# Filters laid out by a copy in DRAM, and an inverse row product summed on VectorE between two exchanges of partitions

## The chip, the core and the metric

One core of one Trainium2 chip. The metric is the device time of one execution in microseconds (us); the median of three runs of the kernel before is 204.33 us (204.27 to 204.45).

## What is computed

The input x has 2048 rows of 640 numbers in bf16. It is normalised row by row; two branches take the normalised rows, and their results are added to x. Branch A is a filter in the frequency domain: a real two-dimensional Fourier transform (2048 x 321 complex values), a product with complex weights w_r + i w_i of that size, and the inverse transform. Branch B is a gated layer with 1536 hidden units.

```python
def _A_ref(x, w_r, w_i):
    X = rfft2(x.astype(float32), axes=(-2, -1))
    X = X * (w_r + 1j * w_i)
    return irfft2(X, s=(S, D), axes=(-2, -1)).astype(bfloat16)

def _B_ref(x, w_gate, w_up, w_down):
    h = einsum("bsd,df->bsf", x, w_gate) * einsum("bsd,df->bsf", x, w_up)
    return einsum("bsf,fd->bsd", h, w_down)

xn = _layernorm(x)
return x + _A_ref(xn, A_w_r, A_w_i) + _B_ref(xn, B_w_gate, B_w_up, B_w_down)
```

## The kernel before

The kernel is a list of tasks, and a planner written in Python orders them before the program is built. Each task has an engine (or a choice of engines), a planned duration, buffers that it reads and writes, and a priority; a lower number is more urgent. The planner (`_Sched.plan`) runs through a model of the five engines, picks the next task by start time and priority, and fixes for every engine the order in which it issues. The chip keeps that order: an instruction that waits on a semaphore holds everything behind it on its engine. All ordinary DMAs are issued from SyncE (SP) by the helper `dma` at L712; evictions of PSUM by ACT or DVE are all recorded at L718 and L719, the two branches of `copy_on`.

Rows are split over partitions as 128 x 16 row blocks b. The work runs in these stages, which overlap:

- *Normalisation.* Statistics of each block, then a subtraction (L824) and a product (L831, task `mul`), in place. From block 4 on, the normalised block is transposed by a DMA within SBUF (L837, issued from SP); the first four blocks are transposed on PE.
- *Branch B, first half.* L978 and L998 multiply the transposed blocks by gate and up weights (five matmuls of 512 columns at L978 for one hidden tile and one of the two weights), ACT or DVE evict, and DVE multiplies the two (L1014). It works on blocks 0 to 3, then 4 to 7, 8 to 11 and 12 to 15. Its priority is 40, so that PE does it whenever nothing more urgent is ready.
- *Branch A, forward.* DVE does a part of the transform along the columns (L891 to L925), PE the next (L938). When all blocks are there, the row stage begins: for t = 0 to 15, two matrices of matmuls (task D, L1056), evictions of 64 partitions, then task C (L1079) with two groups g = 0, 1 of 321 columns each.
- *Filter product, inverse rows.* DVE multiplies C's PSUM output by the filter's real and imaginary part (task WM: two instructions at L1094 and one at L1097 per group) into the buffer Y. The negated parts are made by NG (L1107, on POOL, ACT or DVE) and NS (L1114 to L1116, on POOL). Task IA (L1130, L1131) then needs two accumulating matmuls for each of five parts of each group: one with the product, one with the negated and exchanged product. Its result is evicted into Z2. Y has three buffers.
- *Filters.* For every second t, three or four DMAs for each of w_r and w_i load four frequency rows straight from the weight in DRAM into one of three SBUF slots, repeated and reversed as the 128 partitions need them. They wait for the last block's `mul`.
- *Inverse columns and output.* I (L1159) needs all of Z2; DVE combines (L1183 to L1216). For each block a and half, ACC (L1237) sums branch B's second product over twelve hidden tiles into a PSUM bank, IV (L1249) adds branch A into that bank, FIN (L1257, DVE) adds x, and a DMA stores the half.

Of the kernel before, what the change touches and what calls it, by code (L numbers as in the profile page):

```python
# [398 lines left out]
def _build_tables():  # L399
# [27 lines left out]
    fd = np.zeros((128, 4 * 128 + 130), np.float64)  # L427
# [25 lines left out]
    t["fd"] = _bf16_bits(fd)  # L453
    t["g"] = _bf16_bits(gd)
# [5 lines left out]
    npm = np.repeat(np.arange(2), _S1)  # L460
    nk1 = np.tile(np.arange(_S1), 2)
    n_re = 64 * npm + 2 * nk1
    n_im = n_re + 1
    tf = np.zeros((128, _NQ, 128), np.float64)
    ti = np.zeros((128, _NQ, 2, 64), np.float64)
    for q in range(_NQ):
        k = _rows(q, npm, nk1)
        ph = two_pi * ((s1[:, None] * k[None, :]) % _S) / _S
        c = np.exp(-1j * ph)
        pm = np.broadcast_to(npm[None, :], (64, 64))  # L470
# [9 lines left out]
        ti[n_re, q, 0] = im.real  # L480
        ti[n_im, q, 0] = -im.imag
        ti[n_re, q, 1] = im.imag
        ti[n_im, q, 1] = im.real
# [3 lines left out]


def _rows(q, pm, k1):
    lo = np.where(pm == 0, q, np.where(q == 0, _R // 2, _R - q))  # L490
    return lo + _R * k1
# [11 lines left out]
_WD_LOADS = ((7, 12), (0, 2), (2, 4), (4, 6), (6, 7))  # L503
_FT_ORDER = (7, 8, 9, 10, 11, 0, 1, 2, 3, 4, 5, 6)
# [5 lines left out]
_YS = 1090  # L510
_NY = 3
# [39 lines left out]
def _build(nc, A_x, A_w_r, A_w_i, B_w_gate, B_w_up, B_w_down, out, opts=None):  # L551
# [3 lines left out]
    with es:  # L555
# [6 lines left out]

        sch = _Sched()
# [27 lines left out]
        lay["TI"] = (lay["WD"][0], 16 * 256)  # L591
# [20 lines left out]
        b_y = alloc("Y", _NY * 2 * _YS)  # L612
# [29 lines left out]
        v_w = V("W").rearrange("p (r w n) -> p r w n", r=2, w=2)  # L642
        v_wr = [v_w[:, 0], v_w[:, 1], V("W3").rearrange("p (w n) -> p w n", w=2)]
        b_wr = [(b_w, 0), (b_w, 16), (b_w3, 0)]
# [5 lines left out]
        v_ti = V("TI").rearrange("p (q c n) -> p q c n", q=_NQ, c=2)  # L650
        v_wd = V("WD").rearrange("p (f d) -> p f d", f=12)
        v_fd = V("FD")
        v_g = V("G")
# [11 lines left out]
        v_y = V("Y").rearrange("p (r g n) -> p r g n", r=_NY, g=2)  # L665
        v_tc2 = V("TC").bitcast(_F32).rearrange("p (r s u n) -> p r s u n", r=2, s=5, u=2)
# [19 lines left out]
        v_sd = arena[:, o_stat + 432: o_stat + 448]  # L686
        b_st = sch.buf("st", 10 ** 9, 1)
# [35 lines left out]
        dma("ld_fd", v_fd[:, 0:642], d_fd, 128 * 1284, [(b_fd, None)], prio=0.3)  # L723
# [240 lines left out]
        for ui, (at_, ci, ft0) in enumerate(units):  # L964
# [7 lines left out]
            for u in range(2):  # L972
                ft = ft0 + u
                if nb == 4:
# [10 lines left out]

                    def em_eg4(c, gu=gu, rr=rr, u=u):
                        return copy_on(c, v_gbf[:, rr, u, :], ps[:, bank_of(gu), :])
# [24 lines left out]
            def em_h(c, ft0=ft0, rr=rr, n=n, rows=rows, nb=nb):  # L1012
                if nb == 4:
                    return c.e.tensor_tensor(v_ht[:, ft0, rows], v_gbf[:, rr, 0, :], v_gbf[:, rr, 1, :], _OP.mult)  # L1014
                return c.e.tensor_tensor(v_ht[:, ft0:ft0 + 2, rows], v_gbf[:, rr, :, 0:n], v_gbf[:, rr, :, n:2 * n],
                                         _OP.mult)
            T("H_%d" % ui, "dve", _d_dve_tt16(min(2 * n, 512)), em_h,
# [4 lines left out]
        for q in range(2):  # L1022
            dma("ld_ti%d" % q, v_ti[:, 16 * q:16 * q + 16], d_ti[:, 16 * q:16 * q + 16], 128 * 8 * 512,
                [(b_wd, ("e", 2048 * q, 2048 * q + 2048))], prio=9.0 + 0.3 * q, after=[muls[opts.get("w_after", 15)]])

        for t in range(16):
# [4 lines left out]
            if t % (_WQ // 2) == 0:  # L1031
                q0 = 2 * t
                for w_ in range(2):
                    wv, dw = wvs[w_], v_wr[wr][:, w_]
                    parts = [(dw[0:64], wv[:, q0:q0 + _WQ, :].rearrange("k1 q l -> k1 (q l)").unsqueeze(1).to_broadcast(
                        [_S1, 2, _WQ * 321]), 64 * _WQ * 642)]
                    o_ = 0
                    if q0 == 0:
                        o_ = 1
                        parts.append((dw[64:128, 0:321], wv[:, _R // 2, :].unsqueeze(1).to_broadcast([_S1, 2, 321]), 64 * 642))  # L1040
                    for d_ in range(2):
                        parts.append((dw[64 + d_:128:2, 321 * o_:321 * _WQ].rearrange("p (q l) -> p q l", l=321),
                                      wv[:, _R - q0 - o_:_R - q0 - _WQ:-1, :], 32 * (_WQ - o_) * 642))
                    for i_, (dst, src_, nb_) in enumerate(parts):
                        dma("ld_w%d_%d_%d" % (t, w_, i_), dst, src_, nb_,
                            [(b_wr[wr][0], ("r", b_wr[wr][1] + 8 * w_ + 2 * i_, b_wr[wr][1] + 8 * w_ + 2 * i_ + 2))],
                            prio=9.5 + 0.05 * t, semkey=("w", wr), after=[muls[opts.get("w_after", 15)]])

            eds = []
# [23 lines left out]
            for g in range(2):  # L1073
                q = 2 * t + g
                pg = pq + 0.0005 * g
                ys = 2 * yr + g

                def em_c(c, q=q, g=g, ar=ar):
                    return c.e.matmul(ps[:, bank_of(c.t), 0:_LP], v_tf[:, q, :], v_a[:, ar, 324 * g:324 * g + _LP],  # L1079
                                      start=True, stop=True)  # L1080
                tc = T("C_%d" % q, "pe", _d_mm(_LP), em_c, reads=[(b_a, ("r", 2 * ar, 2 * ar + 2)), (b_tf, ("t", t, t + 1))],
                       prio=pg, bank="single", cls="b")

# [266 lines left out]
```

## Time and profile before

| what | value |
|---|---|
| median of three runs | 204.33 us |
| span of the profiled execution (its own time in the profile) | 202.8 us |
| what the median holds beyond that span | 1.5 us |
| PE, DVE, ACT, POOL busy | 198.0, 179.5, 127.5, 32.0 us |
| bytes moved by DMA | 23.82 MB |
| row stage, from D's first matmul to I's first | 82.6 to 140.1 us |
| first product with a filter (L1094) | 86.5 us |
| first inverse matmul (L1130) | 90.3 us |

The span runs from the first to the last instruction. A busy time is the union of an engine's records; records of PE matmuls overlap, so that the mean of a record (196 ns for 64 columns) is longer than the distance between two. A DMA's time to landing runs from its issue until its data are there. The DMA share is the mean busy share of the core's 16 DMA engines.

### The profile page before, as it was taken

Reading aid. Unit: us, or ns where it says so; the run is one execution under the profiler, and the core shown is the slowest. Engines: PE = TensorE matmul, PEld = TensorE weight load, DVE = VectorE, ACT = ScalarE, POOL = GpSimd, SP = SyncE. Lnnn points to the kernel's source line nnn. Section 1 sums busy time; section 2 is a strip of 40 time slices with the busy share of each in tenths; the row PEclk is TensorE's granted clock in tenths of the full one; section 3 lists DMA queues with packets and bytes.
Section 4 is the critical chain, followed back from the end, with each engine's and each line's share of the span. In section 5 each row is a group of like instructions: output and inputs, shape, how many; then the busy total and the mean of one; then the engine's idle time right before and its main releaser. Section 6 shows DMA issues by size and latency. Waiting matters only on the chain.

```text
span 202.8 us, 4769 instructions
## 1 busy us (share of the span) xinstructions
PE 198.0 (98%) x1785; PEld 128.1 (63%) x1785; DVE 179.5 (89%) x511; ACT 127.5 (63%) x277; POOL 32.0 (16%) x108
## 2 busy tenths in 40 slices
PE   7999999999999999899999999999999999999995
PEld 7987644454444555556666666667777767777774
DVE  3599999999999997697988898864999999999983
ACT  3678899999975776869999999987611220200000
POOL 0000000000000000075754675453000000000000
DMA  6999983031161597605354444004313332332222
GB/s 183 300 341 378 377 80 65 3 65 32 32 63 39 112 276 194 197 14 132 74 145 114 103 102 127 0 5 136 92 32 97 106 107 66 113 90 81 93 65 65
DMA packets 31542, 23.82 MB, mean 117 GB/s; under 512 B 10528, under 2 KB 29472, under 8 KB 31392
## 3 DMA queue, kind: packets, MB, share of 16 engines
q1 hardware_dynamic: 30720, 23.16, 43.5%
q10 hardware_dynamic: 800, 0.36, 0.6%
q8 instruction: 14, 0.23, 0.5%
q14 instruction: 8, 0.07, 0.1%
HBM read 18.92 MB, written 2.62 MB: 106 GB/s over the span
## 4 chain that ended last, share of the span: by engine, by line
PE 85%; DVE 5%; SPq 4%; DMA 4%; issue 1%; ACT 1%
PE ps L978 44%; PE ps L1237 23%; SPq L712 4%; DMA arena<-in_A_x_dram 4%; PE ps L1131 3%; PE ps L1130 3%; PE ps L998 2%; PE ps L1079 2%; PE ps L938 2%; PE ps L1159 2%; PE ps L1249 2%; PE ps L1056 2%; DVE arena L719 1%; DVE arena L1257 1%; DVE arena L1186 0%
## 5 line engine op out<-in xcount | busy, mean ns | idle before, releaser
L718 ACT ACTIVATE arena<-ps 128x512 bf16<-128x512 f32 (+7 forms) x206 | 104.8, 547 | 40.1 <-PE ps L1159 24.0
L978 PE MATMUL ps<-arena 128*128 128x512 bf16 x420 | 97.0, 379 | 0.1
L978 PEld LDWEIGHTS ps<-arena 128*128 128x128 bf16 x420 | 38.9, 98 | 41.9 <-ACT arena L718 1.4
L1237 PE MATMUL ps<-arena 128*128 128x320 bf16 (+2 forms) x396 | 56.5, 295 | 0.2 <-DVE arena L1257 0.2
L1237 PEld LDWEIGHTS ps<-arena 128*128 128x128 bf16 x396 | 37.6, 98 | 13.9 <-DVE arena L1257 0.5
L1094 DVE TENSOR_TENSOR arena<-ps,arena 128x256 bf16<-128x256 f32 x64 | 24.0, 416 | 0.1
L1014 DVE TENSOR_TENSOR arena<-arena 128x512 bf16<-128x512 bf16 x42 | 17.7, 421 | 4.7 <-ACT arena L718 4.7
L1107 POOL TENSOR_SCALAR arena<-arena 128x256 bf16<-128x256 bf16 x8 | 6.8, 855 | 89.3 <-DVE arena L1097 89.2
L719 DVE CAST arena<-ps 64x321 bf16<-64x321 f32 (+1 forms) x25 | 12.2, 490 | 6.3 <-PE ps L1131 5.8
L1257 DVE TENSOR_TENSOR arena<-ps,arena 128x320 bf16<-128x320 f32 (+2 forms) x33 | 15.4, 473 | 1.8 <-PE ps L1249 1.8
L998 PE MATMUL ps<-arena 128*128 128x128 bf16 (+1 forms) x160 | 14.4, 246 | 0.4 <-ACT arena L718 0.4
L1130 PEld LDWEIGHTS ps<-arena 128*128 128x128 bf16 x160 | 12.4, 114 | 2.8 <-ACT arena L718 0.4
L998 PEld LDWEIGHTS ps<-arena 128*128 128x128 bf16 x160 | 12.0, 98 | 2.1 <-ACT arena L718 1.2
L1130 PE MATMUL ps<-arena 128*128 128x64 bf16 x160 | 13.3, 196 | 0.0
L1131 PE MATMUL ps<-arena 128*128 128x64 bf16 x160 | 13.3, 197 | 0.0
L1131 PEld LDWEIGHTS ps<-arena 128*128 128x128 bf16 x160 | 11.2, 113 | 2.1
L1116 POOL TENSOR_SCALAR arena<-arena 128x65 bf16<-128x65 bf16 x32 | 12.1, 378 | 0.0
L1114 POOL COPY arena<-arena 128x63 bf16<-128x63 bf16 x32 | 8.6, 268 | 17.1 <-DVE arena L1097 17.0
L1097 DVE TENSOR_TENSOR arena<-ps,arena 128x130 bf16<-128x130 f32 x32 | 9.3, 292 | 0.0
L776 ACT ACTIVATE arena<-arena 128x640 bf16<-128x640 bf16 x11 | 9.1, 824 | 0.0
L1115 POOL COPY arena<-arena 128x63 bf16<-128x63 bf16 x32 | 9.0, 280 | 0.0
L891 DVE TENSOR_TENSOR arena<-arena 128x384 f32<-128x384 bf16 x16 | 8.8, 552 | 0.0
(62 smaller groups left out, 221.0 us busy)
## 6 DMA issues: line engine op xcount, KB each, us to landing
arena<-in_A_x_dram SPq DMA_DIRECT2D x20, 160.0 KB, 2.4
out_dram<-arena SPq DMA_DIRECT2D x31, 80.0 KB, 1.6
arena<-in_A_w_r_dram SPq DMA_DIRECT2D x8, 160.5 KB, 3.0
arena<-in_A_w_i_dram SPq DMA_DIRECT2D x8, 160.5 KB, 3.0
arena<-in_B_w_gate_dram SPq DMA_DIRECT2D x4, 320.0 KB, 5.8
arena<-in_A_x_dram SPq DMA_DIRECT2D x1, 1280.0 KB, 9.8
arena<-in_A_w_r_dram SPq DMA_DIRECT2D x14, 80.2 KB, 2.9
arena<-in_A_w_i_dram SPq DMA_DIRECT2D x14, 80.2 KB, 3.1
```

The costliest lines, as they stand in the source:

```text
L718: return c.e.activation(dst, src, _ACTF.Copy)
L719: return c.e.tensor_copy(dst, src)
L978: ins = c.e.matmul(ps[:, bk, :], v_gw[:, w, j, ft, :], v_xt[:, j, rows], start=(j == 0), stop=(j == 4))
L998: ins = c.e.matmul(ps[:, bk, w * n:(w + 1) * n], v_gw[:, w, j, ft, :], v_xt[:, j, rows], start=(j == 0), stop=(j == 4))
L1014: return c.e.tensor_tensor(v_ht[:, ft0, rows], v_gbf[:, rr, 0, :], v_gbf[:, rr, 1, :], _OP.mult)
L1094: c.e.tensor_tensor(dst, xh.unsqueeze(1).to_broadcast([128, 2, 32, 4]), wv, _OP.mult)
L1097: return c.e.tensor_tensor(d5, x5, wg[:, :, 0:321:5], _OP.mult)
L1116: return c.e.tensor_scalar(yg[:, 128:193], yg[:, 256:321], -1.0, None, _OP.mult)
L1130: c.e.matmul(dst, l1, v_ti[:, q, 0, :], start=True, stop=False)
L1131: ins = c.e.matmul(dst, l2, v_ti[:, q, 1, :], start=False, stop=True)
L1237: ins = c.e.matmul(ps[:, bk, 0:sl3.stop - sl3.start], v_ht[:, ft, a * 128:(a + 1) * 128], v_wd[:, ft, sl3], start=(ft == _FT_ORDER[0]), st ...
L1257: return c.e.tensor_tensor(v_out[:, a % 2, sl3], ps[:, bk, 0:sl3.stop - sl3.start], v_xr[:, xs, sl3], _OP.add)
```

## The change

The inverse row product becomes one matmul for each part instead of two. What the second matmul did is done ahead of it, on the products. DVE forms the product with the imaginary filter part first (WQ), two DMAs within SBUF move its odd partitions to even ones and back (sw), DVE forms the product with the real part (WP) and adds the moved one (SUM); two more DMAs move the mirrored half across the two halves of the partitions (ng). Then IA runs with half as many matmuls. NG and NS are gone. C and IA handle both groups at once in a pair of PSUM banks, and the eviction of IA takes both groups in one instruction. Y has five buffers of a smaller size; two buffers for moved products lie over others that are no longer in use.

The filters are first rearranged in DRAM: 18 DMAs (wprep) copy w_r and w_i, each row twice, into a tensor w_slots in the order in which the 128 partitions need them. The eight large ones copy 31 x 32 rows of 321 values. They are issued from SP, the first when block 7 is normalised, the next one block later, and so on; the ten small ones after block 15. Their planner priority is 0.5, ahead of the transposes at L837. Loading a slot then takes two DMAs, which wait for all the copies. The imaginary part of each slot gets alternating signs on POOL (WS), from a column of +1 and -1.

At the output, ACT evicts both halves of a block and DVE adds x in one bf16 instruction, with one store for each block; only block 15 keeps the old way. ACC's tasks are placed behind IA of t = 13. The inverse table TI has half its size and W_down is loaded in another split and order. A branch that multiplies out of PSUM (`hu`) is there and not used. The tables are changed to fit. The diff, without the tables:

```diff
-        ti[n_im, q, 0] = -im.imag
-        ti[n_re, q, 1] = im.imag
-        ti[n_im, q, 1] = im.real
+        ti[n_re, q] = im.real
+        ti[n_im, q] = -im.imag
...
     t["ti"] = _bf16_bits(ti)
...
@@ -500,15 +501,16 @@
 _LN_GROUPS = ((0, 1), (1, 1), (2, 1), (3, 1), (4, 2), (6, 2), (8, 2), (10, 2), (12, 2), (14, 2))
 _NGW = 12
...
+        d_w2 = nc.dram_tensor("w_slots", [2, _R // 2, 64, 2, 321], _BF).ap()
...
-        lay["TI"] = (lay["WD"][0], 16 * 256)
+        lay["TI"] = (lay["WD"][0], 16 * 128)
...
-        b_y = alloc("Y", _NY * 2 * _YS)
+        b_y = alloc("Y", _NY * 2 * _YZ)
+        b_qs = alloc("QS", _YZ, at=lay["STAT"][0])
+        b_qs2 = alloc("QS2", _YZ, at=lay["DUM"][0])
...
-        b_wr = [(b_w, 0), (b_w, 16), (b_w3, 0)]
+        v_w = V("W").rearrange("p (r q w l) -> p r q w l", r=2, q=_WQ, w=2)
+        v_wr = [v_w[:, 0], v_w[:, 1], V("W3").rearrange("p (q w l) -> p q w l", q=_WQ, w=2)]
...
+            dma("ld_ti%d" % q, v_ti[:, 16 * q:16 * q + 16], d_ti[:, 16 * q:16 * q + 16], 128 * 16 * 128,
...
+        prep = []
+        for w_ in range(2):
+            for h_ in range(2):
+                for x_ in range(2):
+                    if h_ == 0:
+                        src_ = wvs[w_][:, 1:_R // 2, :].rearrange("k1 q l -> q k1 l")
+                        dst_ = d_w2[0, 1:, x_::2, w_, :]
+                    else:
+                        src_ = wvs[w_][::-1, _R // 2 + 1:_R, :].rearrange("k1 q l -> q k1 l")
+                        dst_ = d_w2[1, 0:_R // 2 - 1, x_::2, w_, :]
+                    prep.append((dst_, src_))
+            z0, z1 = d_w2[0, 0, :, w_, :], d_w2[1, _R // 2 - 1, :, w_, :]
+            for zz, i_, src_ in ((z0, 0, wvs[w_][0:16, 0, :]), (z0, 16, wvs[w_][0:16, _R // 2, :]), (z1, 0, wvs[w_][16:17, 0, :]),
+                                 (z1, 1, wvs[w_][31:16:-1, 0, :]), (z1, 16, wvs[w_][31:15:-1, _R // 2, :])):
+                n_ = src_.shape[0]
+                prep.append((zz[2 * i_:2 * i_ + 2 * n_].rearrange("(i x) l -> x i l", x=2), src_.unsqueeze(0).to_broadcast([2, n_, 321])))
+        prep.sort(key=lambda p_: -math.prod(p_[0].shape))
+        for i_, (dst_, src_) in enumerate(prep):
+            dma("wprep%d" % i_, dst_, src_, 2 * math.prod(dst_.shape), [(b_w2, ("r", i_, i_ + 1))], prio=opts.get("prep_prio", 0.5),
+                semkey=("wp", i_ % 6), after=[muls[min(15, opts.get("prep_after", 7) + int(opts.get("prep_step", 1.0) * min(i_, 8)))]], q=opts.get("prep_q", "sp"))
...
-                for w_ in range(2):
-                    wv, dw = wvs[w_], v_wr[wr][:, w_]
-                    parts = [(dw[0:64], wv[:, q0:q0 + _WQ, :].rearrange("k1 q l -> k1 (q l)").unsqueeze(1).to_broadcast(
...
+                for h_ in range(2):
+                    src_ = d_w2[h_, q0:q0 + _WQ] if h_ == 0 else d_w2[h_, _R // 2 - 1 - q0::-1][0:_WQ]
+                    dma("ld_w%d_%d" % (t, h_), v_wr[wr][64 * h_:64 * h_ + 64].rearrange("p q w l -> p q (w l)"),
+                        src_.rearrange("q n w l -> n q (w l)"), 64 * _WQ * 1284,
+                        [(b_wr[wr][0], ("r", b_wr[wr][1] + h_, b_wr[wr][1] + h_ + 1)), (b_wr[wr][0], ("r", b_wr[wr][1] + 32 + h_, b_wr[wr][1] + 33 + h_))],
+                        prio=9.5 + 0.05 * t, semkey=("w", wr), reads=[(b_w2, None)])
+
+            if t % (_WQ // 2) == 0:
+                def em_ws(c, wi=v_wr[wr][:, :, 1, :]):
+                    return c.e.tensor_scalar(wi, wi, v_tau, None, _OP.mult)
+                T("WS_%d" % t, opts.get("ws_eng", ("pool",)), {"pool": 3400.0, "dve": 470.0}, em_ws, reads=[(b_fd, None)],
+                  writes=[(b_wr[wr][0], ("r", b_wr[wr][1] + 32, b_wr[wr][1] + 64))], prio=9.5 + 0.05 * t)
...
-            for g in range(2):
-                q = 2 * t + g
...
-                def em_wm(c, tc=tc, yr=yr, wr=wr, q=q, g=g):
...
+
+            def em_c(c, t=t, ar=ar):
...
+                ins = None
+                for g in range(2):
+                    ins = c.e.matmul(ps[:, bk + g, 0:_LP], v_tf[:, 2 * t + g, :], v_a[:, ar, 324 * g:324 * g + _LP],
+                                     start=True, stop=True)
+                return ins
+            tc = T("C_%d" % t, "pe", 2 * _d_mm(_LP), em_c, reads=[(b_a, ("r", 2 * ar, 2 * ar + 2)), (b_tf, ("t", t, t + 1))],
+                   prio=pq, bank="pair", cls="b")
+
+            def em_wm(c, w, tc=tc, wg=wg, yb=yb):
+                bk = bank_of(tc)
+                ins = None
+                for h in range(2):
+                    xh = ps[:, bk:bk + 2, 0:256].rearrange("p g (k h m) -> p g h m k", k=4, h=2)[:, :, h]
+                    wv = wg[:, w, :, 0:320].rearrange("p g (m k) -> p g m k", k=10)
+                    wv = wv[:, :, :, 1:5] if h == 0 else wv[:, :, :, 9:5:-1]
+                    d_ = yb[:, :, 322 * w:322 * w + 320].rearrange("p g (h m k) -> p g h m k", h=2, k=5)[:, :, h, :, 1:5]
+                    ins = c.e.tensor_tensor(d_, xh, wv, _OP.mult)
+                return ins
+
+            def em_wq(c, em_wm=em_wm, yb=yb, tc=tc, wg=wg):
+                bk = bank_of(tc)
+                x5 = ps[:, bk:bk + 2, 256:321].unsqueeze(2).to_broadcast([128, 2, 2, 65])
+                d5 = yb.rearrange("p g (w n) -> p g w n", w=2)[:, :, :, 0:321:5]
+                c.e.tensor_tensor(d5, x5, wg.rearrange("p w g l -> p g w l")[:, :, :, 0:321:5], _OP.mult)
+                return em_wm(c, 1)
+            wq = T("WQ_%d" % t, "dve", 1252.0, em_wq, reads=wk, writes=yk(0, 1, 2), prio=pq - 0.001, frees=tc)
+
+            def em_wp(c, em_wm=em_wm):
+                return em_wm(c, 0)
+            wp = T("WP_%d" % t, "dve", 832.0, em_wp, reads=wk, writes=yk(3), prio=pq - 0.001, frees=tc)
+            hold(tc, wq, wp)
...
+            for i_ in range(2):
+                dma("sw%d_%d" % (t, i_), qs[i_:128:2, :, 0:321], yb[1 - i_:128:2, :, 322:643], 64 * 1284,
+                    [(bq, ("r", kq + i_, kq + i_ + 1))], prio=sp_, semkey=("sw", t % _NS), reads=yk(1, 2))
+
+            def em_sum(c, yb=yb, qs=qs):
+                return c.e.tensor_tensor(yb[:, :, 0:321], yb[:, :, 0:321], qs[:, :, 0:321], _OP.add)
+            T("SUM_%d" % t, "dve", _d_dve_tt16(642), em_sum, reads=[(bq, ("r", kq, kq + 4))],
+              writes=yk(0, 3), prio=pq - 0.0015)
...
+            else:
+                mv = [(slice(64 * i_, 64 * i_ + 64), slice(64 - 64 * i_, 128 - 64 * i_), slice(0, 2), 1 + i_) for i_ in range(2)]
+            for i_, (pd, psr, gs, k_) in enumerate(mv):
+                k_ = 16 * yr + 4 * k_ + i_ // 2
+                dma("ng%d_%d" % (t, i_), yb[pd, gs, 321:640], yb[psr, gs, 1:320], 64 * 1276,
+                    [(b_y, ("r", k_, k_ + 1))], prio=sp_, semkey=("ng", yr), reads=yk(0, 3))
...
+            def em_ia(c, t=t, yb=yb):
...
+                for g in range(2):
                     for k in range(5):
-                        if k < 4:
...
-                        c.e.matmul(dst, l1, v_ti[:, q, 0, :], start=True, stop=False)
-                        ins = c.e.matmul(dst, l2, v_ti[:, q, 1, :], start=False, stop=True)
...
+                        o_ = (k + 1) % 5
+                        ins = c.e.matmul(ps[:, bk + g, 64 * k:64 * k + 64], yb[:, g, o_:o_ + 636:5], v_ti[:, 2 * t + g, :],
+                                         start=True, stop=True)
+                return ins
+            ia = T("IA_%d" % t, "pe", 10 * _d_mm(80), em_ia,
+                   reads=yk(0, 1, 2, 3) + [(b_wd, ("e", 128 * t, 128 * t + 128))], prio=pq, bank="pair", cls="b")
+
...
+                src = ps[:, bk:bk + 2, 0:320].rearrange("p g (k m) -> p k g m", m=4)
+                return copy_on(c, v_z2w[:, :, :, t, :].rearrange("p k a (g m) -> p (k a) g m", g=2), src)
+            eia = T("eIA_%d" % t, ("act", "dve"), {"dve": _d_dve_psum(640), "act": _d_act(640)}, em_eia,
+                    writes=[(b_z2, ("t", t, t + 1))], prio=pq - 0.001, frees=ia)
+            hold(ia, eia)
+            ias.append(ia)
...
-                [(b_wd, ("e", 640 * f0, 640 * f1))], prio=18.0 if f0 < 7 else 9.6, after=[muls[opts.get("w_after", 15)]])
+                [(b_wd, ("e", 640 * f0, 640 * f1))], prio=18.0 if f0 < 4 else 9.6, after=[muls[opts.get("w_after", 15)]])
...
-                    kw = dict(bank="single", cls="acc") if own is None else dict(after=[ag2])
+                    kw = dict(bank="single", cls="acc", after=[ias[opts.get("acc_after", 13)]]) if own is None else dict(after=[ag2])
...
-                def em_f1(c, own=own, a=a, xs=xs, sl3=sl3):
...
+                if a >= opts.get("fin_direct", 15):
...
+                def em_f0(c, own=own, a=a, sl3=sl3):
+                    return copy_on(c, v_out[:, a % 2, sl3], ps[:, bank_of(own), 0:sl3.stop - sl3.start])
+                f0 = T("FINA_%d_%d" % (a, hf), opts.get("fin_eng", "act"), {"act": _d_act(c1 - c0), "dve": _d_dve_psum(c1 - c0)}, em_f0,
+                       writes=[(b_out, rb[0])], prio=opts.get("fin_prio", 41.0) + 0.05 * a - 0.001, frees=own, after=[iv])
+                if hf == 0:
...
+                def em_f2(c, a=a, xs=xs):
+                    return c.e.tensor_tensor(v_out[:, a % 2], v_out[:, a % 2], v_xr[:, xs, :], _OP.add)
+                T("FIN_%d" % a, "dve", _d_dve_tt16(640), em_f2, reads=[(b_xr, ("r", xs, xs + 1))],
+                  writes=[(b_out, ro[0])], prio=opts.get("fin_prio", 41.0) + 0.05 * a - 0.001)
+                dma("st_out%d" % a, ov[:, a, :], v_out[:, a % 2], 128 * 1280, [],
+                    prio=pc - 0.003, reads=[(b_out, ro[0])], semkey=("out", a % 2, 0))
```

## Prediction

> **What bounds the kernel now.** I read the engine sums first, then the busy time by stage, the chain that ended last, the waits, and last the queue of DMA issues (SP). The engine line:
>
> ```profile
> PE 198.0 (98%) x1785; PEld 128.1 (63%) x1785; DVE 179.5 (89%) x511; ACT 127.5 (63%) x277; POOL 32.0 (16%) x108
> ```
>
> PE is busy for 198.0 of 202.8 us. That alone isn't proof, since overlapping matmuls are merged, so the stages and the chain come next. Columns: window, its length, busy us of PE, PEld, DVE, ACT, POOL, granted clock, share of the 16 DMA engines, GB/s.
>
> ```profile
> 110.00:120.00 10.00, 10.00 (x124) 6.27 (x122) 9.03 (x30) 9.59 (x24) 6.68 (x22) 1.00 0.34 83
> 120.00:130.00 10.00, 10.00 (x131) 6.42 (x130) 8.11 (x25) 9.62 (x23) 5.34 (x18) 1.00 0.37 91
> 150.00:190.00 40.00, 39.82 (x317) 28.99 (x316) 40.00 (x98) 5.20 (x8) 0.00 (x0) 1.00 0.32 95
> ```
>
> The row stage (82.6 to 140 us) has PE full and ACT at 96%; the output stage has PE and DVE full. In the chain a matmul costs its spacing, not its 196 ns record:
>
> ```profile
> 101.62 0.03 PE ps L1130
> 101.65 0.04 PE ps L1131
> ...
> 102.42 1.08 PE ps L978 x5
> ```
>
> By line the chain gives L1130 and L1131 2.6% each, 10.5 us for 320 matmuls: 33 ns each. A removed inverse matmul is worth 33 ns. The queue of DMA issues matters because the change puts its first step there:
>
> ```profile
> 66.44 1.20 SPq L837 DMA_TRANSPOSE arena<-arena  x1
> 67.69 1.06 SPq L712 DMA_DIRECT2D arena<-c_ti  x2
> 68.79 2.58 SPq L712 DMA_DIRECT2D arena<-in_A_w_r_dram  x4
> ```
>
> Today the filters go straight from DRAM to SBUF. Their issue begins at 68.8, after the last row block is normalised; the first product (L1094) starts at 86.5 and nobody waits for a filter. DMA is never the bound here.
>
> [...] With GpSimd pieces of 0.27 to 0.86 us beside it, the trace shows L1014 at an unchanged 421 ns.
>
> **The change, part by part.**
>
> *Inverse product in one pass.* 160 matmuls go: 160 x 33 ns = 5.3 us of PE in a stage where PE is full. C and inverse take PSUM banks in pairs; bounds -1 to +2 us, I take 0.
>
> *Negations and half copies.* POOL's 96 pieces and 8 of the 32 negations (L1107) leave POOL, 16 negations leave ACT (6.7 us), 8 leave DVE (2.0). In exchange POOL gets 8 sign multiplications (WS) of 1284 elements: from 377 ns at 65 elements and 856 at 256, 2.5 ns per element, 3.4 us each. Only the first stands in line; the later ones have a group time of 6.7 us, [...] 0 to 8 x 3.4 = 27 us, I take 0.
>
> *VectorE products.* The 64 of 256 elements stay (416 ns). 32 of 130 elements (9.3 us) become 16 of 260 (0.42 each, 6.7). 16 sums of 642 bf16 elements are new; L1014 shows 421 ns for 512, so 0.49 each, [...] I take 8. So DVE gets 8 - 2.6 - 2.0 = 3.4 us more in a stage where it idles 10 of 57: hidden.
>
> *Two DMA hops per step.* After the product come two DMAs within SBUF (sw), the sum, then two more (ng) before the inverse matmuls. The nearest landings are 1.6 us (stores) and 2.9 (filter pieces); issue is 0.33 to 0.60 us. I take 2.0 + 2 x 0.5 = 3.0 per hop, bounds 2.3 to 4.1. The path from product to inverse grows from 3.8 us (86.5 to 90.3) to about 1.2 + 3.0 + 0.5 + 3.0 = 7.7. In mid-stage L978 fills PE; at the end it costs up to 3.9 us, less what ACC work covers: I charge 3.8. Without cover for any step it would be 16 x 3.9 = 62 us; five buffers of Y speak against that.
>
> *Eviction and output.* 32 evictions of 320 become 16 of 640: ACT 0.706 against 2 x 0.436, 2 us off ACT, hidden. For 15 row blocks FIN becomes two ACT copies (0.44 each, ACT is 13% busy there) and one DVE sum of 640, about 0.49, for 2 x 0.48: 7 us off DVE. PE is the bound there too: 0. The gate of ACC behind the inverse of t = 13 changes nothing: ACC starts at 138.3 today, later than that. Half as much TI and the other order of W_down: 0, prefetched.
>
> *Filters rearranged in DRAM.* This is the part that decides. Eight copies of 31 x 32 rows of 642 bytes, 7936 rows, 5.09 MB, and ten small ones. The slowest dimension of each large copy, source and destination, is 31, [...] each runs on one DMA engine, [...] Eight serial copies then. The rate of one engine: GB/s over 16 x share, 83 / (16 x 0.34) = 15.3 in the window from 110 us, where mostly these rows are moved, so 42 ns a row. Fast bound: 359 GB/s at share 1.12 (10 to 20 us), 20 GB/s. [...]
>
> The sum, in the profiled execution's time. The first copy waits for the eighth row block (L831, 31.98 + 0.38), so starts at 32.4; 7936 x 42 ns = 333 to 365.7. Small copies: 256 rows with outermost 2, [...] 128 x 42 ns = 5.4; landing 1.5: 372.6. Every filter load waits for all copies and stands in SP's queue: two issues 1.2, landing 3.0, first WS 3.4: 380.2 for the first product. From there today's kernel needs 202.8 - 86.5 = 116.3; less 5.3, plus 3.8: 114.8. Span 495.0; the runs' median lies 1.5 above the span (204.33 - 202.8): 496.5, given as 495.
>
> What else is queued: the transposes of row blocks 7 to 15 follow the copies [...]: block 7 at about 74, blocks 8 to 11 up to 241. PE in its fixed order stops at L978 of blocks 4 to 7, then of 8 to 11; ACT and DVE queue behind it. That adds nothing: the last load is later still. PE work ahead of the first inverse is done in the wait, work behind it is not, since PE keeps its order.
>
> **Rivals.** *Sixteen engines (not slower).* If the copies spread, they take 333 / 16 = 21 us inside 32 to 66; then ten issues of 0.6 to 72.4, landing 2.0, loads 4.2, WS 3.4: 82 us, ahead of 86.5. Then 204.3 - 5.3 + 1.5 (what little of the 3.8 isn't covered) = 200.5, faster. For: the DMA share of 0.29 from 40 to 66 us leaves room. [...] It decides from an aggregate rate of 5.09 MB in (86.5 - 32.4 - 15.7) = 38 us, 132 GB/s, nine engines.
>
> *Sixteen engines, but SP's queue binds.* Four DMAs per step and a load, 5 x 0.60 = 3.0 us of issue; steps come every 3.4 us now and must come every 3.1. At 0.7 an issue costs 3.5 x 16 = 56 us against some 50, and the hops stack at the end: 204.3 - 5.3 + 3.8 + 6 = 209. For: filter issues do take 0.60. Against: x loads take 0.43. It decides from 0.62 us an issue.
>
> **How the numbers follow.** One engine: 0.86; spread and good: 0.08; spread and SP-bound: 0.06. Inside the first, 20 GB/s gives 495 - 78 = 417 [...]. I set 400 to 675, about 93% of that case, so 0.80 in all; the other two cases lie outside and hold 0.14. Times within 0.2% count as the same, about what a measurement here can tell. Faster 0.08, same 0.02, slower 0.90.
>
> **What would show it.** Right: the DMA share near 0.06 (one of 16) for hundreds of us, [...]; PE and DVE idle from some 75 us in stretches that end with transposes; the first products of L1094's successor at about 380; a tail of about 115 us like today's. The steps: inverse spacing 33 ns at half the count, WS 3.4, sum 0.5, hops 3.0. Wrong: a share well above 0.06 during the copies, or a first product before 100 us. [...] the first rival's sum holds. If [...] rows are shorter or longer than 42 ns, only the size is off: 7.9 us for each ns.

## The result and the profile after

The changed kernel takes 476.06 us (median of four runs, 475.23 to 476.81), the kernel before 204.39 beside it: a ratio of 2.328, 95% interval 2.325 to 2.331. The span of the profiled execution is 473.4 us. Engine sums and the chain that ended last:

```profile
PE 206.7 (44%) x1625; PEld 126.5 (27%) x1625; DVE 183.0 (39%) x471; ACT 141.5 (30%) x292; POOL 28.4 (6%) x12
SPq 65%; PE 14%; DVE 11%; DMA 7%; issue 2%; POOL 1%; ACT 0%; POOLq 0%
```

No engine computes for even half of the span, and two thirds of the chain are the queue of DMA issues. The line numbers have moved: the helper `dma` is L721, the transposes are L846, the first half of branch B L987, WS L1085, C L1125, the products L1139 and L1146, SUM L1161, IA L1183. The stages, in the columns of the windows shown of before:

```profile
34.00:66.00 32.00, 3.66 (x23) 1.63 (x20) 7.39 (x21) 4.51 (x11) 0.00 (x0) 0.60 0.07 18
...
110.00:135.00 25.00, 0.00 (x0) 0.00 (x0) 0.00 (x0) 0.00 (x0) 0.00 (x0) 0.50 0.07 18
...
337.10:409.00 71.90, 57.89 (x482) 30.91 (x481) 53.81 (x118) 48.33 (x94) 23.80 (x7) 0.93 0.60 137
409.00:473.40 64.40, 60.54 (x509) 44.77 (x506) 52.51 (x122) 23.32 (x47) 0.00 (x0) 1.00 0.28 88
```

Read the last two columns first. While a copy runs alone, the DMA share is 0.07 at 18 GB/s, about that of one engine of sixteen (1/16 = 0.063). That each copy of 31 outermost runs on one engine was an assumption of the prediction, which no trace of before showed; this trace agrees with it (whether all eight use the same one isn't shown). PE stands still in the second row, and its granted clock is 0.50. In the row stage (337 to 409 us) PE is busy for 57.9 of 71.9 us; before, it was busy for 56.8 of 57.5 there (82.6 to 140.1 us). The output stage differs little: PE is busy for 60.5 of 64.4 us there, and for 60.2 of 62.7 in the stage before (140.1 to 202.8 us).

The issue queue of SP (start, duration, line, copies and transposes in turn):

```profile
32.73 0.83 SPq L721 DMA_DIRECT2D w_slots<-in_A_w_r_dram  x1
33.61 33.48 SPq L846 DMA_TRANSPOSE arena<-arena  x1
...
279.65 0.63 SPq L721 DMA_DIRECT2D w_slots<-in_A_w_i_dram  x1
280.32 34.92 SPq L846 DMA_TRANSPOSE arena<-arena  x1
315.29 3.47 SPq L721 DMA_DIRECT2D w_slots<-in_A_w_r_dram  x3
...
323.09 1.20 SPq L846 DMA_TRANSPOSE arena<-arena  x1
...
325.65 2.67 SPq L721 DMA_DIRECT2D arena<-w_slots  x4
```

A copy's issue takes 0.6 to 0.8 us. The transpose behind it, 1.2 us otherwise, takes 33 to 35: SP itself stands in that instruction, by these times until the copy is nearly through (why it stands there isn't shown). So a copy comes every 35.3 us, which for 992 rows is 35.6 ns a row. The waits of PE (total, times, longest):

```profile
PE ps L987 <- DMA arena<-arena: 146.0, 2, 112.4
PE ps L1125 <- POOL arena L1085: 100.9, 1, 100.9
```

The two stops at L987 are those for the transposes of block 7 and of block 11. The third is C of t = 0: the program holds C back until the other inputs of its products are there too (the helper `hold`), so that C waits for the sign multiplication of the first filter slot. While PE waits, nothing behind the waiting matmul starts: PE has no record in 110 to 135 us (second row of the stages above), inside the stop of 112.4. Then the first product follows:

```profile
337.08 0.88 DVE L1146 TENSOR_TENSOR arena<-ps,arena 128x260 bf16<-128x260 f32 x1 [101.22 <-PE ps L1125]
```

### The profile page after: what moved, and what is told of

It reads as the page before. It is cut to its first block, busy times and chain, and to the rows that moved or that the text cites. A ratio compares the mean times of both kernels' runs of the same rounds, so it can differ in the third digit from the quotient of the medians.

```text
span 473.4 us, 4358 instructions
## 1 busy us (share of the span) xinstructions
PE 206.7 (44%) x1625; PEld 126.5 (27%) x1625; DVE 183.0 (39%) x471; ACT 141.5 (30%) x292; POOL 28.4 (6%) x12
## 4 chain that ended last, share of the span: by engine, by line
SPq 65%; PE 14%; DVE 11%; DMA 7%; issue 2%; POOL 1%; ACT 0%; POOLq 0%
SPq L846 59%; PE ps L1291 10%; SPq L721 6%; DMA arena<-arena 5%; DVE arena L1139 2%; DVE arena L1146 1%; PE ps L987 1%; DMA arena<-w_slots 1%; DMA arena<-in_A_x_dram 1%; PE ps L1303 1%; DVE arena L1028 1%; PE ps L1213 1%; POOL arena L1085 1%; DVE arena L1161 1%; PE ps L1183 1%
## 5 line engine op out<-in xcount | busy, mean ns | idle before, releaser
L727 ACT ACTIVATE arena<-ps 128x512 bf16<-128x512 f32 (+7 forms) x237 | 124.1, 552 | 321.4 <-PE ps L987 271.9
L987 PE MATMUL ps<-arena 128*128 128x512 bf16 x420 | 105.7, 403 | 146.0 <-DMA arena<-arena 146.0
L987 PEld LDWEIGHTS ps<-arena 128*128 128x128 bf16 x420 | 40.3, 102 | 194.1 <-issue 156.7
L1028 DVE TENSOR_TENSOR arena<-arena 128x512 bf16<-128x512 bf16 x42 | 19.2, 456 | 155.4 <-ACT arena L727 155.2
L1291 PE MATMUL ps<-arena 128*128 128x320 bf16 (+2 forms) x396 | 57.4, 295 | 0.2 <-DMA arena<-in_B_w_down_dram 0.2
L1146 DVE TENSOR_TENSOR arena<-ps,arena 128x260 bf16<-128x260 f32 x16 | 14.1, 881 | 102.1 <-PE ps L1125 102.1
L1125 PE MATMUL ps<-arena 128*128 128x321 bf16 x32 | 7.1, 320 | 100.9 <-POOL arena L1085 100.9
L1085 POOL TENSOR_SCALAR arena<-arena 128x1284 bf16<-128x1284 bf16 x8 | 28.2, 3529 | 362.9 <-DMA arena<-w_slots 362.9
L1125 PEld LDWEIGHTS ps<-arena 128*128 128x128 bf16 x32 | 3.1, 102 | 104.3 <-issue 101.9
L1139 DVE TENSOR_TENSOR arena<-ps,arena 128x256 bf16<-128x256 f32 x64 | 24.8, 439 | 2.6 <-PE ps L1125 2.6
L1161 DVE TENSOR_TENSOR arena<-arena 128x642 bf16<-128x642 bf16 x16 | 11.5, 719 | 9.5 <-DMA arena<-arena 9.5
L1183 PE MATMUL ps<-arena 128*128 128x64 bf16 x160 | 9.2, 207 | 10.3 <-DMA arena<-arena 6.4
L1183 PEld LDWEIGHTS ps<-arena 128*128 128x128 bf16 x160 | 8.2, 130 | 14.9 <-DMA arena<-arena 9.5
L1095 PE MATMUL ps<-arena 128*128 128x64 bf16 (+1 forms) x160 | 8.5, 197 | 3.7 <-DVE arena L1139 3.0
L1303 PE MATMUL ps<-arena 128*128 128x320 bf16 (+2 forms) x33 | 8.3, 295 | 0.6 <-DVE arena L1270 0.6
L1330 DVE TENSOR_TENSOR arena<-arena 128x640 bf16<-128x640 bf16 x15 | 7.3, 487 | 3.0 <-ACT arena L727 3.0
```

The costliest lines, as they stand in the source:

```text
L727: return c.e.activation(dst, src, _ACTF.Copy)
L987: ins = c.e.matmul(ps[:, bk, :], v_gw[:, w, j, ft, :], v_xt[:, j, rows], start=(j == 0), stop=(j == 4))
L1085: return c.e.tensor_scalar(wi, wi, v_tau, None, _OP.mult)
L1139: ins = c.e.tensor_tensor(d_, xh, wv, _OP.mult)
L1146: c.e.tensor_tensor(d5, x5, wg.rearrange("p w g l -> p g w l")[:, :, :, 0:321:5], _OP.mult)
L1161: return c.e.tensor_tensor(yb[:, :, 0:321], yb[:, :, 0:321], qs[:, :, 0:321], _OP.add)
```

## Experiments: one engine, and who stands behind it

**Copies of another shape (e1).** Same rows, same bytes, no outer count of 31; their gates are 0.6 of a block apart, since there are twelve large copies now.

```diff
-src_ = wvs[w_][:, 1:_R // 2, :].rearrange("k1 q l -> q k1 l")
-dst_ = d_w2[0, 1:, x_::2, w_, :]
+src_ = wvs[w_][:, 1:_R // 2, :]
+dst_ = d_w2[0, 1:, x_::2, w_, :].rearrange("q k1 l -> k1 q l")
...
+for q0_, q1_ in ((0, 16), (16, 31)):
+    prep.append((d_w2[1, q0_:q1_, x_::2, w_, :],
+        wvs[w_][::-1, _R // 2 + 1 + q0_:_R // 2 + 1 + q1_, :].rearrange("k1 q l -> q k1 l")))
```

> The same rows of 642 bytes and the same bytes are copied, but no copy has an outermost count of 31: the first half goes with 32 outermost, the second half in pieces of 16 and 15. If each copy of 31 ran on one DMA engine, the copies now spread: DMA share well above 0.3 while they run, all of them landed before 90 us, the first product near 83 to 92 us. Then the rest of the change decides: 200.5 by the prediction's first rival, 209 by its second, and 204 + 21 = 225 at most if the whole excess of the tail measured in the changed kernel (136 instead of 115 us) comes with it. If the time lies in the number of rows or bytes and not in the number of engines, the copies still end near 315 us and the time stays at 450 to 480.

Measured: 232.77 us (232.15 to 235.35; ratio to before 1.140, 1.132 to 1.148). One of the copies with 15 outermost, the transpose behind it, and the first product:

```profile
61.96 0.89 SPq L721 DMA_DIRECT2D w_slots<-in_A_w_r_dram  x1
62.90 1.27 SPq L846 DMA_TRANSPOSE arena<-arena  x1
...
93.61 0.88 DVE L1148 TENSOR_TENSOR arena<-ps,arena 128x260 bf16<-128x260 f32 x1
```

So 243 of the 272 us go with the outer count; on how many engines the copies of 32, 16 and 15 run isn't shown. The order of the rows isn't the cause: the first half has another order now, but the second half keeps its own and is only split, and its copies are quick as well. The kernel stays 28 us slower than before, more than any theory allowed: neither rival's sum (200.5, 209) holds either.

**Half of them.** The first half's edit alone: copies 1, 2, 5 and 6 get 32 outermost, the others keep 31.

> Four of the eight large copies get an outermost count of 32, the other four keep 31. By the theory of one engine per copy of 31 four times 35.3 us go: 476 - 141 = 335 us. If engines aren't the cause, 476. If one copy of 31 were enough to spoil it (a single queue with a fixed delay), also near 476.

Measured (one run): 353.47 us, 122.6 less than 476.06 instead of 141. SP's queue shows both kinds side by side:

```profile
33.24 0.73 SPq L721 DMA_DIRECT2D w_slots<-in_A_w_r_dram  x1
34.01 1.33 SPq L846 DMA_TRANSPOSE arena<-arena  x1
...
43.84 0.75 SPq L721 DMA_DIRECT2D w_slots<-in_A_w_r_dram  x1
44.64 34.09 SPq L846 DMA_TRANSPOSE arena<-arena  x1
```

Behind a copy of 32 the transpose takes 1.3 to 3.4 us, behind one of 31 34 to 35. The missing 18 us are the time from each spread copy to the next one: 10.6 us for the first two together (33.24 to 43.84), in which SP also sits idle for 5.8 us until the next row block is normalised, and 7.3 for the other two (114.33 to 121.60).

**Another queue.** The copies as in the changed kernel, issued by ACT: `opts.get("prep_q", "act")`.

> The copies stay as they are, 31 outermost, but ACT issues them, so that SP's queue holds the transposes alone. If order within one queue held the transposes back, they now land by about 70 us, PE doesn't stop between 40 and 70 and between 104 and 212 us, and all of branch B's first half can be done before the filters come: the last filter load still waits for 283 us of copies, the first product stays at 325 to 345, and the time falls by at most what PE no longer has to do after it, some 30 us: 440 to 476. If the transposes are held by the one busy engine itself, whatever the queue, the two long stops of PE stay and the time is 470 to 480. If the prediction's sentence that the late transposes add nothing is exact, 476.

Measured (one run): 477.82 us. Moving the copies doesn't help, and the way in which it doesn't is the point. ACT's records (its DMA issues are ACTq):

```profile
41.16 25.36 ACTq L721 DMA_DIRECT2D w_slots<-in_A_w_r_dram  x1
66.56 0.60 ACT L727 ACTIVATE arena<-ps 128x512 bf16<-128x512 f32 x1 [24.93 <-issue]
66.59 34.90 ACTq L721 DMA_DIRECT2D w_slots<-in_A_w_r_dram  x1
```

Now ACT stands in its next copy until 66.5, as SP stood in the transpose until 67.1. What stands in these two runs is the instruction that issues the next DMA on that queue, for 25.36 and 34.90 us here and for 33.48 there. The transposes, alone on SP's queue here, are held no longer, although the same copies run beside them (durations in ns and times to landing in us, least, median, longest; the median landing in the changed kernel is 38.4 us):

```profile
L846 SPq DMA_TRANSPOSE arena<-arena x12: 1199/1212/1670, 23.9 to 251.8; - x12
DMA to landing us min/median/max: 2.6/6.6/9.2
```

So order within one queue held them (38.4 us against 6.6), and not the busy engine by itself. That the total lies in the range given for the busy engine has another reason. ACT evicts and normalises too, so the row blocks come late, the transposes are issued late (the last at 251.8 us) and PE stops for ACT instead of for a transpose:

```profile
PE ps L987 <- ACT arena L727: 243.9, 7, 67.9
```

The prediction's sentence that late transposes add nothing isn't tried cleanly by this: the filters' wait and a blocked engine are both there.

**Copies that nobody reads.** The kernel before, with the 18 copies as changed, and with the filters loaded as before.

```diff
+d_w2 = nc.dram_tensor("w_slots", [2, _R // 2, 64, 2, 321], _BF).ap()
...
+for i_, (dst_, src_) in enumerate(prep):
+    dma("wprep%d" % i_, dst_, src_, ..., q=opts.get("prep_q", "sp"))
```

> The kernel before, with the 18 copies added as the changed kernel has them, into a tensor that nobody reads; the filters are loaded as before, from the weights. No filter waits for a copy's data. If only that wait cost the time, 204 to 215. If the queue order on SP is enough (transposes of blocks 7 to 15, and the filter loads behind them, stand behind copies that last 35 us each), the last transpose lands near 326, and from there the kernel before needs 202.8 - 91 = 112 us (it reaches blocks 12 to 15 at about 91): 438, and up to 460 with a lower granted clock.

Measured (one run): 455.05 us. No filter waits for a copy's data, and 250 of the 272 us are there. The same transposes of 33 to 35 us stand on SP, the last at 322.46, and the filter loads stand behind it:

```profile
322.46 1.20 SPq L839 DMA_TRANSPOSE arena<-arena  x1
...
324.81 2.58 SPq L714 DMA_DIRECT2D arena<-in_A_w_r_dram  x4
...
333.66 0.75 DVE L1117 TENSOR_TENSOR arena<-ps,arena 128x256 bf16<-128x256 f32 x2 [98.09 <-PE ps L1102]
```

So queue order alone is enough for most of the time; in the changed kernel the wait for the data lies beside it, and no run has that wait without an engine standing behind the copies. The first product (L1117) is at 333.66, and from there this kernel, with the old row product, takes 119.6 us to the end, at a granted clock of 0.98 (before: 116.3; changed: 136.3).

## Experiments: the 28 us that are left

**The copies alone, spread.** The kernel before, with the copies of e1's shape, unread.

> The kernel before with copies of 32, 16 and 15 outermost added, which nobody reads: the price of the copies alone once they are spread. The base of the last four runs (232.8 us) shows a PE stop of 7.3 us at 40 to 50 us behind them. If that stop is all, 204.7 + 7 = 212; if PE has work to put there, 205 to 208; if the copies also delay the filter loads behind them and contention remains, up to 222. What is left of 232.8 - 204.7 = 28 us then belongs to the row product.

Measured: 213.96 us (ratio 1.046, 1.042 to 1.049): 9.3 us. PE stops once for 6.1 us, for a transpose behind a copy, and what stands behind the stop isn't made up; where the other 3 us go isn't shown. So even spread copies aren't hidden.

**The rest of the change, without the copies (e12).** Everything else of the change stays; each slot filled by two DMAs of the same size from other rows of the weights.

```diff
-src_ = d_w2[h_, q0:q0 + _WQ] if h_ == 0 else d_w2[h_, _R // 2 - 1 - q0::-1][0:_WQ]
+src_ = (A_w_r, A_w_i)[h_][512 * (t // 4):512 * (t // 4) + 512].rearrange("(q n w) l -> q n w l", q=_WQ, w=2)
```

> The changed kernel without the copies: each slot is loaded by its two DMAs of the same size from other rows of the weights, so the filters are wrong rows and the output isn't the reference's. Everything else of the row product and of the output stays. By the prediction's terms (5.3 us of PE less, 3.8 us of hops more, all else hidden) 203 to 209; if the 21 us by which the tail exceeded the forecast belong to the row product (hops, SP's issues, GpSimd's lock, VectorE), 218 to 226; if they come from the copies' late end alone, near 204.

Measured: 228.60 us (228.52 to 228.95; ratio 1.117, 1.115 to 1.119): 24 us, just above the highest range given. The output is in it with next to nothing (see the last run), so this is the row product, which I had put at -1.5. Copies and row product, 9.3 + 24, are more than the 28 of both together. PE idles for 20 of 70 us (columns as above), and its two largest waits are those of the inverse matmuls (L1162) for a hop and of the forward columns (L947) for VectorE (total, times, longest):

```profile
80.00:150.00 70.00, 50.05 (x447) 27.18 (x448) 51.56 (x111) 47.40 (x96) 24.59 (x7) 0.93 0.54 122
...
PE ps L1162 <- DMA arena<-arena: 8.1, 4, 4.7
PE ps L947 <- DVE arena L934: 5.3, 1, 5.3
```

Two things stand out in this trace. One is VectorE, while GpSimd multiplies the first two filter slots (its instruction: 75.99 us, 7.43 for two):

```profile
76.26 3.18 DVE L918 TENSOR_TENSOR arena<-arena 128x256 f32<-128x256 f32 x1
...
80.03 3.21 DVE L921 SCALAR_TENSOR_TENSOR arena<-arena 128x256 bf16<-128x256 f32 x1
```

L918 and L921 take 0.42 us otherwise; the 5.3 us of PE for the forward columns follow from this. The other is SP, which from 94.1 to 116.0 us issues 28 DMAs with no gap above 0.05 us:

```profile
94.10 14.65 SPq L721 DMA_DIRECT2D arena<-arena  x17
...
110.80 5.23 SPq L721 DMA_DIRECT2D arena<-arena  x8
```

The 17 are the hops of t = 0 (2 + 7) and of two further steps; their median is 0.61 us and the longest 1.26. At 118.08 a SUM begins that waited 4.0 us for its hop, and IA waited 4.7 at 116.85.

**Hops out, sign out.** The same kernel without sw, ng and WS; SUM adds the product on its own partition, and the first of IA's five parts reads another part's columns.

```diff
-dma("sw%d_%d" % (t, i_), qs[i_:128:2, :, 0:321], yb[1 - i_:128:2, :, 322:643], ...)
-return c.e.tensor_tensor(yb[:, :, 0:321], yb[:, :, 0:321], qs[:, :, 0:321], _OP.add)
+return c.e.tensor_tensor(yb[:, :, 0:321], yb[:, :, 0:321], yb[:, :, 322:643], _OP.add)
-dma("ng%d_%d" % (t, i_), yb[pd, gs, 321:640], yb[psr, gs, 1:320], ...)
-T("WS_%d" % t, ...)
```

> Base: the changed kernel without copies (228.6 us, 24 above the kernel before). The DMAs sw and ng and the sign multiplications on GpSimd are left out as well, so the output isn't the reference's; the products, the sum, the 160 inverse matmuls less and the new output stay. If the two hops with their issues on SP and GpSimd's blocking of VectorE make up the 24 us, 199 to 206, below the kernel before by up to the 5.3 us of matmuls. If the longer products on VectorE and the planned order have a share, the rest stays: 209 to 216. If neither hops nor blocking are on the path, 224 to 229.

Measured: 207.82 us (ratio 1.015, 1.012 to 1.019). Hops and sign together are 20.8 of the 24 us. The 3.1 us that remain lie between the two expectations: even with the hops for nothing the row product isn't faster than before. The first product comes at 86.5 us in the kernel before; here it is without the copies, and then without hops and sign as well:

```profile
92.60 0.89 DVE L1125 TENSOR_TENSOR arena<-ps,arena 128x260 bf16<-128x260 f32 x1
...
85.08 0.88 DVE L1119 TENSOR_TENSOR arena<-ps,arena 128x260 bf16<-128x260 f32 x1
```

It comes 7.5 us earlier in the second. No hop has run by then, so these 7.5 us are not the hops'; of what is left out, only the sign multiplications work ahead of it (the planned order differs a little too). From the first product to the end the difference is 134.6 - 120.9 = 13.7 us, in which hops and sign both have a part. PE idles for 4.6 of 53.5 us, with ACT and DVE at about 90%:

```profile
86.50:140.00 53.50, 48.87 (x477) 28.39 (x477) 47.98 (x118) 48.56 (x98) 0.00 (x0) 1.00 0.37 87
```

**Hops out alone,** from e1 (232.8 us).

> Base: the kernel with copies of 32 outermost (232.8 us). The DMAs sw and ng are left out: SUM adds the product that lies on its own partition, the inverse matmuls read the half that was never moved, so the output isn't the reference's. If the two hops (each some 2.6 us of landing and up to 1.2 us of issue on SP) hold PE in the row stage, the time from the first product to the end falls by the 15 to 21 us that the changed kernel shows beyond the forecast: 210 to 218. If the lock between GpSimd and VectorE, the longer products on VectorE or the planned order hold it, at most 4 us go: 229 to 233.

Measured: 219.9, 225.4 and 228.7 us. The three scatter too widely to give the hops a figure; all lie below e1. In the profiled execution, the longest of the three, DVE is busy for 58.5 of 60 us (90 to 150), GpSimd for 27.1: without hops, but with GpSimd's sign multiplications, VectorE is nearly full; how much of it is blocking isn't shown. This experiment doesn't divide the 20.8 us between hops and sign.

**Three repairs that failed,** each from e1 (232.77 us); all three end above every range given for them. First, WS on VectorE, `ws_eng` = ("dve",).

> Base as before (232.8 us). The eight sign multiplications of the filters (WS) go from GpSimd to VectorE. In the base's trace five VectorE instructions that overlap one on GpSimd last longer than their median: sums of 3.03 and 1.79 instead of 0.49 us, H of 3.14, 1.19 and 1.05 instead of 0.42, together 8.2 us more. If this blocking is on the path, up to 8 us go, and 3.5 - 0.5 = 3.0 us ahead of the first product as well: 222 to 228. If VectorE has cover, or the eight instructions of some 0.4 to 1.4 us put on it cost as much as they save: 231 to 236.

Measured: 239.18 us (237.06 to 239.74). GpSimd is busy for 0.00 us from 30 us to the end, so no instruction of it runs beside one of VectorE, but VectorE now stands for the loads:

```profile
DVE arena L1087 <- DMA arena<-w_slots: 15.5, 8, 4.0
```

Second, the first hop issued by ACT: `q="act"` at sw.

> Base as before (232.8 us). The first hop's DMAs (sw, two per step) are issued by ACT instead of SP. If SP's issue time (in the base 17 DMAs stand in a row for 17 us, 1.0 us each) binds the row stage, halving its load brings 5 to 12 us: 221 to 228. If the landing of 2.6 us and the order bind, nothing: 231 to 234. If 32 issues of 0.6 us (19 us) on ACT, which evicts PE's banks, cost more than they give: 235 to 245.

Measured: 247.43 us (245.77 to 248.65). The issue of sw needs the product, and ACT's evictions stand behind it. The wait line of those evictions names VectorE's product:

```profile
ACT arena L727 <- DVE arena L1141: 13.3, 4, 3.8
```

So whether SP's issues or the landing cost more in a hop isn't told by this run; that SP is full is read from traces only. Third, all copies behind the last transpose: `after=[muls[15]]`, priority 8.0.

> Base as before (232.8 us). All copies wait for the last row block and stand behind the transposes on SP's queue, instead of between them from block 7 on. If transposes behind copies in one queue cost the PE stop of 7.3 us at 40 to 50 us, this stop is gone; the copies then run from about 68 us and take 18 issues of 0.6 to 1.0 us and 5.09 MB at full spread, so that the first product comes at 95 to 100 instead of 94 us: 224 to 229. If the first product moves with the copies, to 105 us or later, the gain is lost: 232 to 240.

Measured: 259.50 us. The stop at 40 us is gone; in its place PE waits for the first slot:

```profile
PE ps L1127 <- POOL arena L1087: 31.0, 2, 30.5
```

The copies have the DMA engines nearly to themselves here, and that gives the speed of spread copies (the DMA share of 1.21 is above 1, so packets' records overlap in it):

```profile
72.00:96.00 24.00, 21.45 (x140) 10.43 (x137) 12.97 (x32) 15.78 (x29) 0.00 (x0) 1.00 1.21 139
```

139 GB/s is 7.7 times the 18 of one engine, not 16 times. The three edits change the planned order too, so the waits are shown, and not that the edits would fail in every order.

**The output alone.** The kernel before, with ACT's copies, the bf16 sum and one store per block.

> The kernel before with one part of the change only: the output (two ACT copies and one VectorE sum of bf16 per block, one store, block 15 as before). By the prediction it takes 7 us off VectorE in a stage where PE is the bound and gives 0: 203.9 to 205.1. If VectorE, full in the output stage as well, holds PE there, 1 to 4 us go: 201 to 203.5. If the longer way from IV over ACT and VectorE to the store holds banks, 206 to 210.

Measured: 204.37 us against 204.69 (11 and 14 runs; ratio 0.9979, 0.9969 to 0.9990). This part is worth 0.2 to 0.6 us, and makes the one version that is ahead of both kernels, by 0.1 to 0.3%. DVE is busy for 175.0 us (before 179.5), ACT for 139.4 (127.5); in the output stage (150 to 190 us) PE is busy for 40.00 of 40 us and DVE still for 39.49.

## Why the prediction was right, and where its sum was off

The forecast was 495 us, measured 476. The main mechanism named, eight serial copies that keep one engine busy (share 0.07 at 18 GB/s), was the one at work: without the outer count of 31, 243 of the 272 us are gone. The sum, term by term:

| step of the prediction | forecast, us | measured, us |
|---|---|---|
| first copy starts | 32.4 | 32.7 |
| eight copies, one after the other | 333.3 (42 ns a row) | 282.6 (35.6 ns) |
| small copies, to the first filter load | 6.9 | 10.4 |
| load, sign, first product | 7.6 | 11.4 |
| first product to the end | 114.8 | 136.3 |
| span | 495.0 | 473.4 |

Two terms were off by much, with opposite signs, so that the forecast came within 4% of the result partly by luck.

- **Row time.** 15.3 GB/s came from a window of mixed transfers on all engines; one engine at work moves 18.0. 7936 rows x 6.4 ns = 51 us too much. The upper end of the range, 675 us, was the author's estimate; no trace of before shows a slow bound for one engine.
- **From first product to the end.** This is the step that failed: "In mid-stage L978 fills PE; at the end it costs up to 3.9 us". The unread copies separate what the change adds: with the old row product the same late start leaves 119.6 us, 3.3 more than before; the new one leaves 16.7 more again; and I had taken 1.5 off. 16.7 + 3.3 + 1.5 = 21.5. The longer time lies in the row stage: from the first product to the first inverse matmul along the columns (I) it is 74.1 us, 53.6 before. The cover isn't there: PE idles for 14 of 72 us in the changed kernel's row stage, and for 20 of 70 without copies.
- **Inverse matmuls.** The 5.3 us were counted at a spacing of 33 ns, and this spacing was a sign to look for. The ten that are left in a step come 39 ns apart (0.39 us to the next task, in the run without hops and sign), so that by this estimate 320 x 33 - 160 x 39 ns = 4.3 us are gained and not 5.3:

```profile
101.36 0.55 PE L1140 MATMUL ps<-arena 128*128 128x64 bf16 x10
101.75 0.71 PE L1098 MATMUL ps<-arena 128*128 128x321 bf16 x4
```

- **Hops.** Size a little low but inside the bounds (3.0 forecast; landing 2.5 and 2.8, two issues of 0.61: 3.7 to 4.0), cover wrong. The second rival's mechanism, SP's queue, "decides from 0.62 us an issue": an issue takes 0.61 to 0.65 with the gap to the next, and SP is seen full for 22 us. As a total this rival was still too low (209): the blocking, at 0 in its sum, and the copies, 9.3 us, are not in it.
- **Blocking of VectorE by GpSimd**, also called a lock in the expectations: taken as 0 of 0 to 27 us. The trace of after shows VectorE instructions that last longer beside a sign multiplication:

```profile
342.71 3.53 POOL L1085 TENSOR_SCALAR arena<-arena 128x1284 bf16<-128x1284 bf16 x1 [2.99 <-DMA arena<-w_slots]
...
343.02 3.12 DVE L1161 TENSOR_TENSOR arena<-arena 128x642 bf16<-128x642 bf16 x1 [0.57 <-DMA arena<-arena]
```

  A sum of 0.50 us (median) lasts 3.12, until about when GpSimd's 3.53 end (346.24). Four more are like it, two sums of 1.05 and 0.89 us and two instructions at L1028 of 1.08 and 1.20 (median 0.42); all five end at most 0.2 us before GpSimd's, and together they last 5.0 us longer than their medians. The product at 388.13 us (L1146), beside GpSimd's of 387.99, keeps its 0.90. That the small pieces of before, 0.27 to 0.86 us, showed nothing was no evidence for pieces of 3.5.
- **VectorE's products.** Sums 0.499 us (median), forecast 0.49. The 260-element product has a record of 0.88 and takes 0.64 to the next start, forecast 0.42; 16 x 0.22 = 3.5 us more.
- **Loads and sign.** The two loads of the first slot land after 5.3 and 6.1 us, forecast 3.0, with four loads of 321 KB and W_down in flight at once; WS 3.5, forecast 3.4.
- **Transposes.** That they land late and that PE stops in blocks was right: PE resumes at about 71 us (forecast 74) and 213 (241). The reason was half right: the order of one queue holds them, as the copies on ACT's queue show (median landings of 38.4 and 6.6 us), but that SP, or ACT, stands in the issue itself, for 25 to 35 us, wasn't in the forecast. That it "adds nothing" is right only for the total, since the filter loads stand behind the same transposes; by the unread copies this queue order alone gives 455 us.
- **Output: 0.** 0.3 us gained between the medians where 0 was forecast; DVE falls by 4.5 us, forecast 7.
- **First rival.** Sixteen engines, 21 us for the copies: they are 7.7 times as fast and not 16 times, so about 37 us, and cost 9.3; with the row product's 24 this rival could not have come out faster. Their 139 GB/s are above the 132 by which it was to be decided, and still the first product came at 93.6 us and not ahead of 86.5: the filter loads are issued only at 81.0, behind the copies and the last transposes, where they were issued at 68.8 before.

What stays open: how the 13.7 us after the first product divide between hops, their issue on SP, and the sign on GpSimd; where the last 3.1 us of the row product come from (the spacing of 39 ns is worth 1.0, VectorE's longer product and the planned order are candidates, not shown); how much of the longer tail is the granted clock, 0.93 in the row stages in which PE idles, where it was 1.00 before; and why spread copies are only 7.7 times as fast.

## What to carry to other kernels

Before a DMA is added, look at the slowest dimension of both its sides: 31 there left 5 MB at 18 GB/s and a DMA share of 0.07, and outer counts of 32, 16 and 15 took 243 us away (no large copy had another count, and why the count decides isn't shown). Then ask what is issued next on the same queue, because the issuing engine itself may stand behind it, 33 to 35 us a copy on SP here, whoever needs the data. And a change that trades matmuls for a round trip over DMA has to be priced with the trip twice per step and the queue's issue time, 4 x 0.65 us here, against the 0.27 us that ten matmuls fewer in a step are worth.

## What was not expected of the hardware

- The issue of a DMA behind a copy of 992 rows with 31 outermost held the issuing engine for 25 to 35 us, on SP and, in the run with ACT's queue, on ACT; behind a copy of 32 outermost in the run with half of them 1.3 to 3.4 us.
- Copies of 31 outermost moved rows of 642 bytes from DRAM to DRAM at 18 GB/s and a DMA share of 0.07; copies with outer counts of 32, 16 and 15 together moved 139 at 1.21.
- A VectorE product of 260 elements, written five apart, from PSUM lasted 0.88 us, one of 130 elements 0.29 in the kernel before, one of 256 in runs of four 0.42.
- The granted clock of TensorE was 0.50 in windows of the changed kernel in which PE does nothing (110 to 135, 140 to 170 and 180 to 205 us), and 0.93 on average over the row stage after them (337 to 409 us).
